# Key-value state and turned query weights through PSUM, large buffers at multiples of 512 bytes, and a new operation list, in a layer of linear attention and gated feed-forward

## The chip, the core and the metric

The kernel runs on one core of a Trainium2 chip. A core has five engines that each work through their own instructions in order: TensorE (PE, matrix products into PSUM, with a second row PEld for its weight loads), VectorE (DVE), ScalarE (ACT), GpSimd (POOL) and SyncE (SP), which here only issues transfers. SBUF is the working memory of 128 partitions; PSUM holds the results of matrix products in eight banks of 128 x 512 float32. The metric is the device time of one execution in microseconds (us); lower is better.

## What is computed

With `xn = layernorm(x)` for 2048 tokens of width 512:

```python
qkv = (xn @ wqkv) -> q, k, v            # 32 heads of 16
phi(t) = [softmax(t @ w_phi), softmax(-t @ w_phi)]        # 32 features per head
kv  = phi(k)^T v                        # per head, 32 x 16
z   = sum over tokens of phi(k)
o   = (phi(q) kv) / (phi(q) z + 1e-6)
s   = o @ wo
g   = silu((relu(xn @ W_gate) * (xn @ W_up)) @ W_down)    # inner width 1376
out = x + s * g
```

## The kernel before

Every matrix product is made in float32 precision from three products of rounded parts: an operand is split into a high part (a rounded copy, made by ScalarE with `activation(..., AF.Copy)`) and a low part (the rest, made by a subtraction on VectorE or GpSimd). The projections and the gate products use block sums in the manner of Strassen (the names P1 to P7 and the six operand blocks A11, S1 and so on).

The work runs in this order. First a front: tokens are loaded, normalised, transposed on TensorE (`pxT`) and split into the large tile XT; the key weights are folded with `w_phi` (`pfold`). Then the keys, values and queries of all tokens, with the sums `pkv` over tokens kept in four PSUM banks. Then the state: the sums are gathered into `kvacc`, turned on TensorE (`pkb`), masked, and split into a high and a low part that lie in XT in the place of block A21 (which the names of the profile therefore call XT). From there TensorE runs the gate products of the first half of the tokens (names ga, gc, gd and the bank `seed`; eleven slices g0 to g10 of the inner width, seven groups of six products each), the down products (`py`) and the query products (`pnum`). In between stand the query steps: fetch and transpose a query tile into a PSUM bank (`pq<-pql`), its bounds (`mx`), shifting (`eq<-pq,mx`), exponentials, sums, normalising, then a turn by VectorE, a split of the turned weights into `pTh` and `pTl`, and two products per query half against the state. After the first half's outputs (`pso`), the second half of the tokens repeats gate, down and query work with code that this change leaves alone (names pa, pb, pc, pd, u, e).

Two things set the order. Up to the end of the first half's gate work it is a list of names, `ORDER` (before line 37 on), which `Plan.run` (line 105) walks through: each name is an operation that issues a few instructions on one engine, and the engines keep this program order. Behind it, the second half is interleaved by a planner's clock (`Clock.pump`). Names in the list that matter here: `Fk0` to `Fk3` fold the key weights, `khN`/`klN` split a fold into its high and low part, `kcN` copies it; `pk1.0` is the first product of key tile 1; `kpN` turns a quarter of the state, `ktN` masks it, `khN_` and `klN_` split it; `qxQ.J` turns half J of query pair Q, `qhQ.J` and `qoQ.J` split it, `qkQ.Ja` multiplies it; `gF.i` is a group of gate products; `put...` stores prepared weights; `xr...` reloads a block of XT for the second half.

Tiles come from rotating sets. PSUM has one bank `seed` and a set of seven (`ps`); a new tile takes a bank over from an older one and its first writer waits until the last reader of the older one is done. SBUF has sets of 2 (`u8`, 8 KB a partition), 24 (`u4`, 4 KB) and 14 (`u2`, 2 KB) buffers. A set is laid out in memory where it is first used. In the kernel before, XT begins at byte 16,896 of a partition and `u2` at 82,432, both multiples of 512; `u8` and `u4` follow some small tiles and begin at 112,832 and 129,216, both 192 bytes past a multiple of 512.

All engine calls go through `InOrder`, so one line (L128 before, L130 after) stands for every instruction in the profile, and they are told apart by the names of their tiles.

Of the kernel before, what the change touches and what calls it, by code (L numbers as in the profile page):

```python
# [38 lines left out]
kc0 ld2 T1 pk0.0 lk3 lv0 lo3 kh2 bn2 kh1 kl1 pk3.0 ld4 kc1 hi1 pw2 kc2 Fk3 lq0 td1 lv1 bi2 pk0.1 ap2 lq1 vh_0
vh_1 vl_0 kl2 sums0 kh3 pk3.1 st4 T2 th1.0 th1.1 lo1 kc3 vh_2 pk0.2 vl_1 pk3.2 pk1.0 kl3 pk0.3 td3 sums1 vl_2  # L40
ep4 hi2 mx0 Fq0 ld5 pk1.1 pw4 Fq1 pk1.2 pk3.3 qh0 tl1.0 ld6 vh_3 sh0 qh1 lo2 pk1.3 pv1.0 ql0 mx3 st5 Fq2 pk2.0
ql1 pv1.1 ex0 ld7 Fq3 qh2 st6 ld9 pk2.1 qh3 mx1 ql2 bi4 ap4 sh1 sm0 lpm pv1.2 ex1 vl_3 pk2.2 sps1 st7 tl1.1 ep5
ql3 pv0.0 sc0 pk2.3 td2 ep7 sps0 ld12 sh3 pv1.3 vh1 pv0.1 pw5 ep6 bi5 td4 ph0 q1.0 th2.0 z0 ex3 pw7 pq1.0 ap5
q2.0 ld10 pv2.0 sm1 sc1 pw6 T5 pv0.2 st9 pq2.0 vl1 ph1 T4 hi5 bi7 sm3 spill0 pv3.0 bi6 ep9 sc3 pv2.1 pv0.3 th2.1
sums2 pl0 ld8 ap6 lo5 pv3.1 ld11 pw9 tl2.0 pv2.2 ap7 hi4 T7 pv3.2 hS2 z1 tl2.1 vh0 th3.0 th3.1 q1.1 mx2 pl1 hi7
st8 lo4 vl0 T6 pq1.1 P1.2 slo2 sh2 sums3 tl3.0 ex2 q2.1 spill1 ep8 cS2 st10 pv2.3 P6.2 pw8 P3.2 hS3 lo7 bankc
sm2 pq2.1 tl3.1 sc2 bankb hi6 slo3 bankd bi9 lo6 sq1.1 ep10 z2 th4.0 banka pw10 pv3.3 ap9 kv0 sq2.0 cU2 vh2 mx4
tl4.0 th4.1 ld13 vl2 bi8 bi10 P7.2 kv1 cW2 P5.2 sh4 ph2 aw2 tl4.1 pl2 vh3 sq2.1 P4.2 z3 vl3 mx5 P2.2 st11 ph3
ap8 ex4 au2 sh5 sm4 P1.3 kv2 q3.0 ap10 cS3 P6.3 ex5 st12 P3.3 sc4 sm5 pq3.0 vh5 sc5 pl3 ep11 T9 pw11 cU3 vl5 hi9
z5 P7.3 T8 mx6 kv3 spill2 cW3 lo9 P4.3 hi8 ph5 spill3 st13 sq1.0 sums4 lo8 hS4 ph4 P5.3 pl5 sh6 ep12 aw3 mx7  # L50
slo4 q3.1 ex6 bi11 pq3.1 ap11 P2.3 pw12 ld15 sh7 P1.4 ex7 sm6 au3 kv5 z4 pl4 cS4 P6.4 vh4 st15 cU4 vl4 sm7 sc6
vh7 sc7 T10 ep15 hi10 ep13 P3.4 P7.4 bi12 z7 vl7 T11 lo10 sums5 pw13 cW4 hi11 kv4 ph7 hS5 P4.4 mx8 lo11 mx9 q4.1
sh9 pq4.1 spS2 pl7 P5.4 aw4 ph6 sh8 bi13 ex9 P1.5 z6 kv7 sm9 P2.4 ld14 cS5 pw15 slo5 au4 P6.5 ex8 ap13 q4.0 P3.5
vh6 sm8 sc8 vh9 st14 cU5 pq4.0 T13 ap12 P7.5 ph8 hi13 sq4.1 sc9 pl6 cW5 spS3 bi15 mx10 T12 vl6 kv6 vl9 hi12 ph9
lo13 sums6 sh10 hS6 lo12 P4.5 z8 ap15 ep14 pl8 z9 mx11 ex10 vh8 q5.1 q5.0 pq5.1 pl9 sm10 slo6 sh11 vl8 pq5.0
sc10 pw14 P5.5 rw0 P1.6 z10 ex11 cS6 aw5 sm11 kv9 P2.5 bi14 fd0 P6.6 rd0 fs0 kv8 ft0 sc11 ap14 T15 au5 ph10 cU6
z11 pl10 T14 hi15 ph11 P7.6 lo15 P3.6 sums7 cW6 mx12 P4.6 vh11 sq3.1 hi14 q6.1 pl11 lo14 mx13 hS7 P1.7 vl11 sh13
pq6.1 kv11 ex13 slo7 cS7 fdl0 sh12 vh10 P5.6 fa0 sm13 P6.7 ex12 P3.7 aw6 rw1 sc13 sm12 P2.6 au6 vl10 kv10 sq5.1
vh13 cU7 ph13 fal0 vl13 fs1 fa1 sq6.1 sc12 fb0 ph12 P7.7 cW7 P5.7 z13 sq3.0 aw7 mx14 vh12 q7.1 fd1 sh14 ft1 P4.7
rd1 mx15 fc0 rw2 pq7.1 P2.7 sq7.1 ex14 q6.0 fbl0 au7 vh14 vl12 fc1 rd2 q8.0 pq6.0 sh15 g0.0 pl13 sm14 sq5.0 fs2  # L60
vh15 sc14 fcl0 ex15 pl12 gt0 sm15 vl15 vl14 kv12 z12 rw3 sq4.0 fs3 g0.1 sq6.0 ph14 sc15 pq8.0 rd3 fb1 q8.1 pq8.1
gm0 g0.2 pl14 kv13 ql0.0 ge0 sq8.0 ql0.1 g0.3 gf0 g0.4 fal1 kv14 g0.5 ph15 fcl1 z15 pl15 g0.6 gp0 fe0 ft2 fbl1
putwa0 gs0 kv15 z14 g1.0 gn0 gg0 fe1 fb2 ka q7.0 qt0.1 g1.1 putwd0 hc0 qm0.1 fel1 kb ft3 kp3 qt0.0 gt1 pq7.0
g1.2 putwa1 fa3 qm0.0 fbl2 ha0 putwb0 fc2 kp1 g1.3 gm1 kt3 ge1 kh3_ fd2 hb0 kp0 qs0.1 fa2 g1.4 kt1 sq7.0 fc3 zp0
fb3 fel0 gf1 qs0.0 sq8.1 kt0 fd3 fe3 fdl1 gp1 qe0.0 g1.5 zc0 fal2 zp1 g1.6 fcl2 ql1.0 kh0_ qt1.0 rw4 gs1 qa0.0
putwb1 kh1_ g2.0 qm1.0 putwc2 g2.1 ha1 of_3 zc1 kl3_ qe0.1 qs1.0 ql1.1 gt2 putfe1 fdl2 gn1 kp2 fel3 putwb2 hd0
g2.2 gg1 fs4 gm2 fdl3 hb1 qt1.1 putwd1 fcl3 putwc1 qe1.0 g2.3 oh_3 hc1 ge2 dn013 kl0_ rd4 kt2 g2.4 fal3 qw0.1
kl1_ fbl3 dn010 kh2_ qm1.1 g2.5 fd4 of_0 qw0.0 hd1 gf2 putwc3 g2.6 fe2 qa0.1 qb0.1 putfe3 putwc0 kl2_ gp2 ow_3
dy010 qs1.1 putwa2 rw5 fa4 gs2 dn012 dy013 g3.0 dn011 os_3 g3.1 qr0 dn000 fal4 dy012 gn2 gt3 g3.2 rd5 qw1.0 fel2
qb0.0 putwa3 dn003 gg2 dy011 fa5 qd0 oh_0 g3.3 dy000 putwa4 ft4 fc4 qa1.0 gm3 ge3 qn0.1 qe1.1 dn002 ow_0 fcl4  # L70
fb4 qx0.1 of_2 gf3 fal5 oh_2 fdl4 qa1.1 g3.4 qn0.0 dn001 qh0.1 g3.5 qx0.0 qh0.0 fbl4 qw1.1 dy003 fs5 putfe0 g3.6
qo0.1 ha2 gp3 gn3 g4.0 rw6 dy001 dy002 putwd3 gt4 qk0.10 qo0.0 ft5 g4.1 qk0.11 fs6 os_0 gg3 qb1.1 gm4 hc3 qc0.10
g4.2 hc2 ge4 fa6 hb2 g4.3 putwd2 qk0.00 qc0.11 g4.4 qb1.0 hd2 hd3 gs3 qr1 rd6 gf4 qk0.01 qd1 g4.5 ow_2 qc0.01
ha3 g4.6 gp4 gn4 dn100 qz0.1 g5.0 rw7 qn1.0 fc5 fd6 fb5 dy100 dn102 fbl5 ql2.0 g5.1 gg4 hb3 qx1.0 gt5 fcl5 fa7
qn1.1 qt2.0 fd5 os_2 dn103 g5.2 of_1 fal7 gm5 dy102 dy103 g5.3 fdl5 putwb4 oh_1 ow_1 ft6 dn101 fs7 fdl6 ge5
qc0.00 putwc5 fc6 rd7 fal6 g5.4 qx1.1 qm2.0 qz0.0 ft7 fb6 dn113 fcl6 dy101 os_1 g5.5 gf5 dn112 qs2.0 putwa5
putwb3 fbl6 dy113 qh1.1 qe2.0 fb7 rw8 putwd4 fd7 fe4 g5.6 qo1.1 gp5 fe5 g6.0 gs5 fel4 qk1.11 g6.1 putwd5 dy112
# [1430 lines left out]
```

## Time and profile before

| | |
|---|---|
| median of 3 runs | 585.66 us (585.11 to 586.7) |
| the profiled execution | 583.23 us |
| its span, first to last instruction | 581.5 us |
| mean granted TensorE clock | 0.991 of full |
| busy PE / PEld / DVE | 561.5 / 462.9 / 427.7 us |
| busy ACT / POOL | 290.0 / 429.6 us |
| moved by transfers | 136.14 MB |

A row of the timeline gives the start (us from the start of the span), the time from the first start to the last end of the merged instructions, engine, line, operation, output<-inputs, shapes, the count, and in brackets how long the engine sat idle before and what ended that. Matrix products are pipelined, so one group's end overlaps the next one's start; their pace is read from start to start. A row of the groups gives busy time and mean ns of one instruction, then the idle time before them. Busy shares of PE are not shares of its peak.

### The profile page before, as it was taken

To read this page: it belongs to the slowest core of one execution; us is meant where nothing else is said; L and a number is where in the kernel's file an instruction comes from. 1 tells how busy PE (TensorE), PEld (TensorE's weight loads), DVE (VectorE), ACT (ScalarE), POOL (GpSimd) and SP (SyncE) were. 2 spreads that over 40 slices of the span, in tenths; PEclk is the share of its full clock that TensorE was granted. 3 is DMA by queue.
4 is the path that set the end of the run, shared out by engine and by line. 5 is a ranking of instruction groups with operands and counts; after the bars stand their busy time and mean duration, and the time that the engine had idled before them with its cause. 6 is when DMAs were issued, how large, how long until landed. Compare 5 with 4: busy or idle time off the path is not lost.

```text
span 581.5 us, 8022 instructions
## 1 busy us (share of the span) xinstructions
PE 561.5 (97%) x2618; PEld 462.9 (80%) x2618; DVE 427.7 (74%) x609; ACT 290.0 (50%) x511; POOL 429.6 (74%) x325
## 2 busy tenths in 40 slices
PE   7899999999999499999979999999999999999997
PEld 6788888888887388888868888878888888888886
DVE  5797898977849998989964543499994969774323
ACT  4899777856547236436353223123564453634510
POOL 1968676879899758879988724362968888888475
PEclk9999999999999789999999999999999999999999
DMA  8654765654786486789899999999666766549883
GB/s 303 233 174 124 185 154 121 143 145 129 215 243 193 161 258 235 227 265 305 305 338 276 346 388 405 399 330 355 176 193 193 235 200 198 169 125 331 223 234 135
DMA packets 81562, 136.14 MB, mean 234 GB/s; under 512 B 7408, under 2 KB 34416, under 8 KB 80624
## 3 DMA queue, kind: packets, MB, share of 16 engines
q1 hardware_dynamic: 77920, 122.97, 63.3%
q0 software_dynamic: 3456, 12.58, 11.4%
q8 instruction: 21, 0.34, 0.2%
q14 instruction: 21, 0.17, 0.1%
q10 hardware_dynamic: 144, 0.07, 0.0%
HBM read 73.47 MB, written 53.74 MB: 219 GB/s over the span
## 4 chain that ended last, share of the span: by engine, by line
PE 89%; issue 3%; DVE 2%; DMA 2%; ACT 2%; POOL 2%; SPq 0%; POOLq 0%; DVEq 0%; ACTq 0%
PE py L128 20%; PE seed L128 9%; PE pa L128 8%; PE pd L128 8%; PE pq L128 8%; PE pso L128 8%; PE pc L128 5%; PE gd L128 5%; PE ga L128 4%; PE gc L128 4%; PE pkv L128 3%; PE pnum L128 3%; PE pv L128 2%; PE pk L128 1%; DMA cb<-cst 1%
## 5 line engine op out<-in xcount | busy, mean ns | idle before, releaser
L128 PE MATMUL py<-fd,hh 128*128 128x512 f32 x528 | 132.8, 395 | 0.0
L128 PEld LDWEIGHTS py<-fd,hh 128*128 128x128 f32 x528 | 100.0, 190 | 22.2
L128 DVE TENSOR_TENSOR y<-py,y 128x512 f32<-128x512 f32 x40 | 26.8, 684 | 24.7 <-PE py L128 24.5
L128 POOL TENSOR_TENSOR phl<-ek,phl 128x1024 fp32r<-128x1024 f32 x16 | 40.5, 2552 | 5.5 <-ACT phl L128 5.5
L128 PE MATMUL pso<-wo,oh 128*128 128x512 f32 (+1 forms) x136 | 39.8, 377 | 0.0
L128 POOL TENSOR_TENSOR ol<-of,oh 128x1024 fp32r<-128x1024 f32 x8 | 19.2, 2400 | 27.6 <-ACT oh L128 17.7
L128 POOL TENSOR_TENSOR ez<-eq,zB 128x1024 f32<-128x1024 f32 x16 | 38.4, 2408 | 0.1
L128 PE MATMUL ga<-XT,wa 128*128 128x512 f32 x132 | 34.4, 396 | 0.0
L128 PE MATMUL pa<-XT,wa 128*128 128x512 f32 x132 | 34.2, 393 | 0.0
L128 PE MATMUL seed<-XT,wb 128*128 128x512 f32 x132 | 34.0, 393 | 0.0
L128 POOL TENSOR_TENSOR y<-y,ys 128x512 f32<-128x512 f32 x24 | 31.1, 1302 | 1.9 <-ACT ys L128 1.9
L128 POOL TENSOR_TENSOR hh<-e,hh 128x512 fp32r<-128x512 f32 x11 | 14.3, 1304 | 24.0 <-ACT hh L128 24.0
L128 DVE TENSOR_TENSOR y<-pso,y 128x512 f32<-128x512 f32 (+1 forms) x15 | 9.8, 656 | 27.6 <-PE pso L128 27.6
L128 PEld LDWEIGHTS pa<-XT,wa 128*128 128x128 f32 x132 | 24.7, 188 | 5.6
L128 PEld LDWEIGHTS ga<-XT,wa 128*128 128x128 f32 x132 | 24.5, 188 | 5.6 <-issue 0.5
L128 PE MATMUL gd<-XT,wc 128*128 128x512 f32 x66 | 18.6, 421 | 10.6 <-DVE eq L128 7.8
L128 PEld LDWEIGHTS seed<-XT,wb 128*128 128x128 f32 x132 | 24.6, 188 | 5.3
L128 PEld LDWEIGHTS pso<-wo,oh 128*128 128x128 f32 x136 | 25.0, 188 | 4.7
L128 ACT ACTIVATE eq<-pnum 128x512 f32<-128x512 f32 x32 | 17.7, 592 | 18.7 <-PE pnum L128 18.7
L128 POOL TENSOR_TENSOR lr<-lr,mhalf 128x1 f32<-128x1 f32 x16 | 9.8, 614 | 22.2 <-DVE lr L128 22.2
L128 ACT ACTIVATE eq<-eq 128x512 f32<-128x512 f32 x32 | 18.4, 623 | 15.2 <-DVE eq L128 15.0
L128 PE MATMUL pso<-wo,ol 128*128 128x512 f32 (+1 forms) x68 | 25.6, 377 | 0.0
(237 smaller groups left out, 1661.5 us busy)
## 6 DMA issues: line engine op xcount, KB each, us to landing
zacc<-ek POOLq DMA_DIRECT2D x16, 512.0 KB, 4.8
XT<-xts SPq DMA_DIRECT2D x7, 1024.0 KB, 17.1
rawg<-wf SPq DMA_DIRECT2D x11, 512.0 KB, 4.9
ws<-wa SPq DMA_DIRECT2D x22, 256.0 KB, 4.6
ws<-wb SPq DMA_DIRECT2D x22, 256.0 KB, 5.7
ws<-wc SPq DMA_DIRECT2D x22, 256.0 KB, 4.8
ws<-fd SPq DMA_DIRECT2D x22, 256.0 KB, 5.6
wa<-ws SPq DMA_DIRECT2D x22, 256.0 KB, 3.1
```

Source lines behind the costliest of these rows:

```text
L128: return self.tc.keep_in_program_order(op(*a, **k))
```

## The change

Four edits.

1. The state. The masked quarter `kvt`, a tile of `u2` in SBUF, goes: the mask is multiplied into the PSUM bank `pkb` in place, and the high copy (ScalarE) and the low subtraction (VectorE) read that bank.
2. The turned query weights of the first half (three query pairs, two halves each). Where VectorE turned 1024 columns from SBUF into a tile `ez` in SBUF, it now turns twice 512 columns into a PSUM bank `pT`; each bank is then split by its own copy on ScalarE and its own subtraction on VectorE.
3. The sets `u8`, `u4` and `u2` are touched right behind XT, before the small tiles, so that they begin at 82,432, 98,816 and 197,120 bytes, multiples of 512.
4. A new `ORDER`, with names for the two parts of each turn.

```diff
+    for buffer in (u8, u4, u2):
+        buffer((P, 512), "first")
...
             def masked():
-                T[t_] = u2((P, 2, P), "kvt")
-                nc.vector.tensor_tensor(T[t_], T[b_], T["pm"][:, 2:4, :], op=ALU.mult)
+                nc.vector.tensor_tensor(T[b_], T[b_], T["pm"][:, 2:4, :], op=ALU.mult)
 
             def high():
-                nc.scalar.activation(kvhl[:, 0, g, :], T[t_], AF.Copy)
-                nc.scalar.activation(quarter(kvhl[:, 1, g, :]), quarter(T[t_]), AF.Copy)
+                nc.scalar.activation(kvhl[:, 0, g, :], T[b_], AF.Copy)
+                nc.scalar.activation(quarter(kvhl[:, 1, g, :]), quarter(T[b_]), AF.Copy)
...
             op(f"kl{i}_", lambda: add(nc.vector, kvhl[:, 1, g, :].rearrange("p q (s c) -> p (q s) c", s=2)[:, 1:3, :],
-                                      quarter(T[t_]), f32(quarter(kvhl[:, 0, g, :])), ALU.subtract), t_)
+                                      quarter(T[b_]), f32(quarter(kvhl[:, 0, g, :])), ALU.subtract), b_)
...
-        def high():
-            T[th] = u4((P, 1024), "pTh", F32R)
-            nc.scalar.activation(T[th], T[ez], AF.Copy)
-
-        def low():
-            T[tl] = u4((P, 1024), "pTl", F32R)
-            add(nc.vector, T[tl], T[ez], f32(T[th]), ALU.subtract)
...
-        op(f"qx{q}.{j}", lambda: nc.vector.transpose(T[ez], flat(T[es])), es, ez)
-        op(f"qh{q}.{j}", high, ez, th)
-        op(f"qo{q}.{j}", low, ez, th, tl)
+
+        def turned(d, p):
+            c = slice(d * 512, (d + 1) * 512)
+
+            def turn():
+                T[p] = ps(name="pT")
+                nc.vector.transpose(T[p], flat(T[es])[:, c])
+
+            def high():
+                if th not in T:
+                    T[th] = u4((P, 1024), "pTh", F32R)
+                nc.scalar.activation(T[th][:, c], T[p], AF.Copy)
+
+            def low():
+                if tl not in T:
+                    T[tl] = u4((P, 1024), "pTl", F32R)
+                add(nc.vector, T[tl][:, c], T[p], f32(T[th][:, c]), ALU.subtract)
+            op(f"qx{q}.{j}{d}", turn, es, p)
+            op(f"qh{q}.{j}{d}", high, p, th)
+            op(f"qo{q}.{j}{d}", low, p, th, tl)
+        for d in range(2):
+            turned(d, f"pT{q}.{j}{d}")
...
 ORDER = """
-ld3 bn3 ld0 pw3 ld1 bn0 bn1 pw0 bi3 ap3 ap0 lk0 lcb T0 pw1 bi1 lk2 Fk0 lk1 T3 Fk2 ap1 hi0 Fk1 lo0 kh0 kl0 hi3
+ld1 ld0 bn1 ld3 bn0 lk0 pw1 bi1 bn3 lcb ap1 lk2 T1 pw0 ap0 pw3 bi3 ap3 T0 Fk0 kh0 sums0 hi1 lk1 lk3 kl0 T3 hi0
```

What the new list moves, at the three places that the prediction speaks of. First VectorE at the state, in the kernel before. `XT<-kvt,XT` is the low subtraction of a state quarter, `kvt<-pkb,pm` the mask, and `eq<-pq,mx` the shifting of a query half, which is the last reader of the bank `pq`.

```order
L128 TENSOR_TENSOR gc<-gc,m 128x512
L128 STREAM_TRANSPOSE pq_2047<-pql 128x512
L128 SCALAR_TENSOR_TENSOR y<-gc,y 128x512
L128 TENSOR_REDUCE qs<-eq 128x64
L128 TENSOR_REDUCE mx<-pq_2047 128x32 x2
L128 TENSOR_TENSOR XT<-kvt,XT 128x128
L128 TENSOR_TENSOR eq<-pq_2047,mx 128x1024
L128 TENSOR_TENSOR m<-gd,m 128x512
```

The same place on VectorE in the changed kernel:

```order
L130 TENSOR_TENSOR gc<-gc,m 128x512
L130 TENSOR_TENSOR XT<-pkb,XT 128x128
L130 SCALAR_TENSOR_TENSOR y<-gc,y 128x512
L130 TENSOR_TENSOR pkb<-pkb,pm 128x256
L130 STREAM_TRANSPOSE pq_2031<-pql 128x512
L130 TENSOR_TENSOR m<-gd,m 128x512
L130 TENSOR_TENSOR pkb<-pkb,pm 128x256
L130 TENSOR_TENSOR XT<-pkb,XT 128x128
L130 SCALAR_TENSOR_TENSOR m<-ga,m 128x512
L130 TENSOR_TENSOR XT<-pkb,XT 128x128
L130 TENSOR_REDUCE mx<-pq_2031 128x32 x2
```

The subtraction of the state reads `pkb` in place of `kvt`, and stands before the transpose that fills the query bank or between it and its bounds, no longer right ahead of the shifting.

Second ScalarE in the front, before. `B21h<-pfold` is the high copy of a key fold (kh2, then kh3), `wkf<-pfold` its full copy (kc), `junk` the statistics of a token tile, `T1h` a split that is needed later.

```order
L128 ACTIVATE wkf<-pfold 128x512
L128 ACTIVATE xt<-xt,lb,lr 128x512
L128 ACTIVATE B12h<-wvr 128x512 x2
L128 ACTIVATE B21h<-pfold 128x512
L128 ACTIVATE junk,lm<-xt 128x512
L128 ACTIVATE junk,lv<-xt,lm 128x512
L128 ACTIVATE T1h<-wkf 128x512 x2
L128 ACTIVATE wkf<-pfold 128x512
```

And in the changed kernel:

```order
L130 ACTIVATE B21h<-pfold 128x512
L130 ACTIVATE wkf<-pfold 128x512
L130 ACTIVATE B21h<-pfold 128x512
L130 ACTIVATE wkf<-pfold 128x512
L130 ACTIVATE B12h<-wvr 128x512
L130 ACTIVATE xt<-xt,lb,lr 128x512
L130 ACTIVATE junk,lm<-xt 128x512
L130 ACTIVATE junk,lv<-xt,lm 128x512
L130 ACTIVATE wkf<-pfold 128x512
```

Both high copies now come ahead of the statistics; in the list the low part kl3 stands before the last full copy kc3, where before it stood behind it.

Third VectorE at the first turned query half, in the changed kernel. `pT<-eq` is a turn of 512 columns into a PSUM bank, `pTl<-pT,pTh` the subtraction that is the bank's last reader.

```order
L130 STREAM_TRANSPOSE pT<-eq 128x512 x2
L130 TENSOR_TENSOR m<-gd,m 128x512
L130 TENSOR_TENSOR pTl<-pT,pTh 128x512
L130 TENSOR_REDUCE qs<-eq 128x64
L130 TENSOR_TENSOR m<-seed,t 128x512
L130 STREAM_TRANSPOSE pT<-eq 128x512
```

And before:

```order
L128 STREAM_TRANSPOSE ez<-eq 128x1024
L128 TENSOR_TENSOR y<-gd,y 128x512
L128 TENSOR_REDUCE qs<-eq 128x64
L128 TENSOR_TENSOR eq<-eq,qr 128x1024
L128 STREAM_TRANSPOSE ez<-eq 128x1024
L128 TENSOR_TENSOR pTl<-ez,pTh 128x1024
```

Where one turn and one subtraction of 1024 columns between SBUF tiles stood, there are now two of each with a PSUM bank between them, and other work of VectorE stands between the turn and the subtraction.

More of the change, by code (lines that the diff above doesn't have):

```diff
@@ L37 @@
 ORDER = """
-ld3 bn3 ld0 pw3 ld1 bn0 bn1 pw0 bi3 ap3 ap0 lk0 lcb T0 pw1 bi1 lk2 Fk0 lk1 T3 Fk2 ap1 hi0 Fk1 lo0 kh0 kl0 hi3
[L39 to L77, printed above, removed]
@@ new lines @@
+ld2 lv0 lo1 Fk2 lo0 Fk1 kc2 kh1 Fk3 hi3 pk1.0 kl1 ld4 pk0.0 kh2 kc0 kh3 bn2 lq0 pk1.1 pw2 kc1 kl2 pk0.1 vh_0 bi2
+pk0.2 kl3 lo3 pk0.3 ap2 st4 mx0 kc3 pk1.2 vh_1 ep4 lq1 sh0 T2 pk3.0 vl_0 td1 hi2 sums1 ex0 lv1 pw4 ld6 pk1.3 Fq0
+lo2 pk3.1 Fq2 qh0 bi4 th1.0 ld5 vh_2 ld7 ql0 qh2 vl_1 pk3.2 Fq1 ql2 pv1.0 pk2.0 tl1.0 ld8 vl_2 Fq3 vh_3 vl_3 sm0
+ap4 pv1.1 pk2.1 st5 qh1 pv1.2 pk3.3 pk2.2 qh3 mx1 sps0 sh1 td3 th1.1 ld9 st6 ld11 ql3 pv1.3 ql1 ex1 T4 ep5 sc0
+ld10 ep6 pk2.3 td2 st7 sm1 pw5 q1.1 bi5 tl1.1 sc1 ld14 z0 pw6 ph0 ep7 mx2 ap5 q2.0 pq1.1 T5 sh2 ld13 pw7 vh1 st8
@@ new lines @@
+hi4 pl0 pq2.0 ph1 bi7 vl1 ex2 td4 sums2 bi6 mx3 hS2 q2.1 ap7 z1 sps1 lo4 pv3.0 q1.0 pq2.1 hi5 sq2.0 sm2 pv3.1
+pv2.0 th2.0 ep8 pv0.0 ap6 pv2.1 slo2 th2.1 pq1.0 pl1 sh3 T6 lo5 pv0.1 ex3 T7 th3.0 pv0.2 sc2 th3.1 sm3 hi6
+spill1 st9 sums3 P1.2 pv0.3 tl2.0 spill0 pv2.2 pv3.2 cS2 hi7 sc3 sq2.1 vh0 st11 spS2 P3.2 bankc lo6 hS3 tl2.1
+bankb tl3.0 lo7 P6.2 banka vl0 cU2 ep9 bankd pw8 pv3.3 tl3.1 kv0 mx4 vh3 th4.0 vl3 th4.1 z3 bi8 ep11 ph3 pv2.3
+slo3 kv1 pw9 sh4 ex4 tl4.0 P7.2 q3.0 cW2 bi9 sm4 tl4.1 vh2 vl2 P4.2 pl3 P5.2 kv3 sq1.0 ap9 sc4 sq1.1 ph2 mx5 ap8
@@ new lines @@
+sq8.1 kp1 fa3 ge1 qm0.1 fe1 putwb1 fcl1 fb2 fdl1 g1.3 kt1 g1.4 fc3 kt0 g1.5 fc2 qs0.1 fel1 z14 ql2.0 kh1_ gf1
+gp1 qe0.0 kp2 rd3 kl1_ fcl2 gs1 fd2 ql1.1 g1.6 kt2 kp3 qt2.0 fbl2 g2.0 ha1 rw4 gn1 kt3 putwa1 putwa0 rd4 fel0
+of_1 kh2_ kh0_ hc0 kl0_ g2.1 gg1 gt2 kl2_ ql1.0 fcl3 fb3 zp1 qm2.0 fdl2 putfe0 g2.2 hb1 putwc0 gm2 zc1 zp0 g2.3
+qa0.0 ge2 putwc3 fal3 rw5 fd4 g2.4 qs2.0 zc0 qt1.0 gf2 qt1.1 g2.5 qm1.0 fbl3 fs4 qs1.0 fe3 qe0.1 putwb3 g2.6 hd0
+gp2 ft4 fa4 gn2 gs2 hc1 oh_1 qw0.1 dn010 g3.0 putwd0 hd1 dy010 kh3_ fd3 putwd1 qb0.1 fdl3 gt3 fs5 putwc1 qm1.1
@@ new lines @@
+putfe7 gt8 dn213 g8.1 fe6 g8.2 putwb8 fs9 putwc8 putfe5 dy213 g8.3 ft9 gm8 qh2.01 qo2.00 gs7 qz1.1 ge8 hd5
+qx2.11 putwd8 qo2.01 dn211 oa0 putwa8 g8.4 qk2.01 fb9 qk2.00 putfe4 fc9 dy211 qc2.01 g8.5 fal9 gf8 dn212 fbl9
+ql3.1 rw10 gp8 fcl9 hd4 qx2.10 qh2.10 qo2.10 dy212 ol1 sg1 sw0 qh2.11 putwd9 fs10 g8.6 qc2.00 qo2.11 g9.0 gt9
+qk2.11 qk2.10 qc2.11 rd10 ft10 sl1 fa10 qc2.10 g9.1 dn210 putwa9 gm9 qz2.0 fc10 fb10 ha7 g9.2 gn8 dn201 qz2.1
+ge9 g9.3 fbl10 hc6 gg8 fcl10 g9.4 g9.5 gs8 sw1 gf9 putwc9 ol2 g9.6 putwb9 gp9 fal10 hb7 dn203 g10.0 hc7 dy201
@@ L92 @@
+fel6 dn310 gs9 dn312 gt10 hc8 wl2 ha8 g10.1 dy210 oa2 hb8 gn9 wl1 fe8 hd6 dn200 hd7 wl0 dy310 fe9 g10.2 gg9 gm10
+xrA11 dn202 ge10 oa1 hc9 g10.3 dy312 xrS2 ha9 dn313 dy203 fe10 dy202 hd8 g10.4 gp10 fel9 fel8 dn303 fd10 g10.5
+dn311 gf10 xrS3 fdl10 gs10 g10.6 dy200 dn300 dy313 xrS1 gn10 xrA22 gg10 ha10 xrS4 dy311 dy300 hd9 xrA12 hb10
+dy303 fel10 hb9 dn302 dn301 wl3 hc10 dy302 putwa10 hd10 dy301 putfe9 putwd10 putwb10 putfe6 putfe8 putfe10
+putwc10
 """
@@ L1067, in kv_part @@
         def kv_part(i):
-            g, b_, t_ = slice(2 * i, 2 * i + 2), f"pkb{i}", f"kvt{i}"
+            g, b_ = slice(2 * i, 2 * i + 2), f"pkb{i}"
             def turn():
```

48 lines of the change are left out of this document (32 added, 16 removed).

## The prediction

> **What bounds the kernel now.** I read the page first, then TensorE's waits, then the timeline at each place where TensorE stops, and last the groups, for the price of each operation that the diff touches. Busy time and the granted clock, from the page:
>
> ```profile
> PE 561.5 (97%) x2618; PEld 462.9 (80%) x2618; DVE 427.7 (74%) x609; ACT 290.0 (50%) x511; POOL 429.6 (74%) x325
> PEclk9999999999999789999999999999999999999999
> ```
>
> TensorE is busy 97% of the span; the span of 581.5 less 561.5 leaves 20.0 us idle in the whole run. No other engine passes 74%. The clock row is low in slices 13 and 14 only, which are 189 to 218 us. Is there anything to gain in the pace itself? The longest stretch of pure products:
>
> ```profile
> 336.31 20.58 PE L128 MATMUL py<-fd,hh 128*128 128x512 f32 x90
> ```
>
> 20.58 / 90 is 229 ns, and a gate group of six takes 1.38 us start to start (below), 230 ns each. So the pace is even, and the change makes no product fewer: a gain must come from idle time. TensorE's waits say where it lies:
>
> ```profile
> PE gd L128 <- DVE eq L128: 7.8, 1, 7.8
> PE gd L128 <- ACT eq L128: 2.8, 1, 2.8
> ...
> PE pnum L128 <- DVE pTl L128: 0.3, 1, 0.3
> ```
>
> One wait of 7.8 us, one of 2.8, and of the turned query weights only 0.3. Here is the first, in TensorE's timeline:
>
> ```profile
> 189.53 1.54 PE L128 MATMUL seed<-XT,wb 128*128 128x512 f32 x6
> 190.91 0.61 PE L128 MATMUL pkb<-pm,kvacc 128*128 128x128 f32 x4
> 191.27 1.64 PE L128 MATMUL gc<-XT,wb 128*128 128x512 f32 x6
> 200.67 2.93 PE L128 MATMUL gd<-XT,wc 128*128 128x512 f32 x6 [7.76 <-DVE eq L128]
> 203.40 2.77 PE L128 MATMUL py<-fd,hh 128*128 128x512 f32 x6
> 205.96 1.80 PE L128 MATMUL gc<-XT,wc 128*128 128x512 f32 x6
> 207.60 0.62 PE L128 MATMUL py<-fd,hh 128*128 128x512 f32 x2
> ```
>
> From seed to the next group it is 190.91 - 189.53 = 1.38, the undisturbed pace. From gc to gd it is 200.67 - 191.27 = 9.40: 8.02 lost. The next three groups take 2.73, 2.56 and 1.64 where 1.38 is due, at the low clock: 1.35 + 1.18 + 0.26 = 2.79 more. The place costs 8.02 + 2.79 = **10.81 us**. What held `eq`, on VectorE:
>
> ```profile
> 188.45 11.03 DVE L128 TENSOR_TENSOR XT<-kvt,XT 128x128 fp32r<-128x128 f32 x1
> 199.41 1.21 DVE L128 TENSOR_TENSOR eq<-pq,mx 128x1024 f32<-128x1024 f32 x1
> ```
>
> `XT<-kvt,XT` is kl2_, one subtraction of 128 columns. It lasts 11.03 us. `eq` queues behind it, is the last reader of a bank of `pq`, and gd needs that bank. And beside it, on GpSimd:
>
> ```profile
> 187.65 1.44 POOL L128 TENSOR_TENSOR tab<-rawg 128x256 f32<-128x256 f32 x2
> ...
> 197.00 2.34 POOL L128 TENSOR_TENSOR ez<-eq,zB 128x1024 f32<-128x1024 f32 x1
> 202.98 1.30 POOL L128 TENSOR_TENSOR hh<-m,hh 128x512 fp32r<-128x512 f32 x1 [3.64 <-ACT hh L128]
> ```
>
> No GpSimd row from 187.65 to 197.00 is marked idle, and the first pause runs from 202.98 - 3.64 = 199.34. The subtraction ends at 188.45 + 11.03 = 199.48. So it stood as long as GpSimd worked without a pause, and ended when the pause came.
>
> **The state, part by part.** The groups price a subtraction with both operands in SBUF, and one with an operand in PSUM:
>
> ```profile
> L128 DVE TENSOR_TENSOR XT<-kvt,XT 128x128 fp32r<-128x128 f32 x4 | 13.1, 3272 | 0.0
> ```
>
> ```profile
> L128 DVE TENSOR_TENSOR y<-py,y 128x512 f32<-128x512 f32 x40 | 26.8, 684 | 24.7 <-PE py L128 24.5
> L128 DVE TENSOR_TENSOR qr<-qr,qd 128x128 f32<-128x128 f32 x8 | 2.4, 299 | 0.3
> ```
>
> `y<-py,y` reads PSUM and SBUF forty times, at all hours of GpSimd, and its mean is a plain 684 ns. `qr`, a bank of PSUM by the code, is the shape at hand: 299 ns for 128 columns. The edit puts `pkb` (PSUM) in the place of `kvt`, so each of the four subtractions should cost 0.3: 13.1 - 4 x 0.3 = 11.9 us off VectorE, of which the 11.03 - 0.3 = 10.7 of kl2_ lay on the path. What is late next? Had kl2_ taken 0.3, `eq` would start at 188.8 and end at 190.0 (1.21 later); gd is due at 191.27 + 1.38 = 192.65. The bank comes 2.7 us ahead, so the stall goes whole, and with it the low clock that followed it: **-10.8**. Bounds: 0 (nothing freed) to -10.81. The mask writes `pkb` in place, and the bank is held until kl, a few more operations; nothing in the trace shows the price, and I put it with the banks below.
>
> The Trainium skill ("SBUF — State Buffer", section "SBUF: two separate sides") says that VectorE with two SBUF inputs and GpSimd exclude each other, the one that starts first holding the ports for one whole instruction. By that, kl2_ could wait for a single GpSimd instruction, 2.34 us at most in these rows; the trace has 11.03, through some nine of them, and the measurement decides. The rule taken at its word is a rival below.
>
> **The front.** TensorE, VectorE and ScalarE at the fold of the keys:
>
> ```profile
> 19.20 0.40 PE L128 MATMUL pk<-B21h,XT 128*128 128x512 f32 x1
> ...
> 21.16 0.50 PE L128 MATMUL pk<-B21l,XT 128*128 128x512 f32 x1 [1.56 <-DVE B21l L128]
> ```
>
> ```profile
> 20.42 0.69 DVE L128 TENSOR_TENSOR B21l<-pfold,B21h 128x512 fp32r<-128x512 f32 x1 [2.08 <-ACT wkf L128]
> ```
>
> ```profile
> 19.81 0.58 ACT L128 ACTIVATE wkf<-pfold 128x512 f32<-128x512 f32 x1
> ```
>
> Start to start 1.96 where 0.23 is due: 1.73 lost to kl3, which on VectorE stands behind kc3's copy on ScalarE, itself behind the statistics and `T1h`. In the new list kl3 stands ahead of kc3, and both high copies ahead of the statistics. I take **-1.7**; bounds 0 (another late operand takes its place) to -1.73.
>
> **The turned query weights.** Price per half, before:
>
> ```profile
> L128 DVE STREAM_TRANSPOSE ez<-eq 128x1024 f32<-128x1024 f32 x16 | 19.8, 1236 | 0.1
> ```
>
> ```profile
> L128 DVE STREAM_TRANSPOSE pq<-pql 128x512 f32<-128x512 f32 x16 | 11.4, 710 | 0.0
> ```
>
> ```profile
> L128 DVE TENSOR_TENSOR pTl<-ez,pTh 128x1024 fp32r<-128x1024 f32 x6 | 9.6, 1601 | 2.4 <-PE pnum L128 1.3 <-ACT pTh L128 0.7 <-PE py L128 0.4
> ```
>
> ```profile
> L128 ACT ACTIVATE pTh<-ez 128x1024 fp32r<-128x1024 f32 x16 | 16.7, 1052 | 1.6 <-POOL wd L128 1.6
> L128 ACT ACTIVATE eq<-pnum 128x512 f32<-128x512 f32 x32 | 17.7, 592 | 18.7 <-PE pnum L128 18.7
> ```
>
> VectorE paid 1236 + 1601 = 2837 ns for each of six halves. Now it pays two turns into PSUM (the `pq` row, 710) and two subtractions from PSUM (the `y` row, 684): 2788. ScalarE paid 1052, and now pays 2 x 592 = 1184 (the `pnum` row reads PSUM). That is 0.3 us less in all on VectorE and 0.8 more on ScalarE, which is busy 50%. TensorE waits 0.3 us in all for `pTl` and never for `pTh`, so I cost this at nothing; the cover is the gate products that stand between. If that cover were gone, a half would gain, not lose: the first bank is turned, copied and subtracted in 710 + 592 + 684 = 1986 ns against 3889 before. Its danger is the bank itself: twelve more tiles go through the set of seven, which is the slower rival.
>
> **Alignment.** No product or wait of before shows its price. The `py` row has both its operands in the buffers that lay 192 past a multiple (`fd` and `hh` are `u4`), while the gate products read XT, which was aligned, and both run at 229 to 230 ns. So I take **0**. One bound is the granted clock: at the low clock six products took 2.56 us, 427 ns each, so full clock could in the end mean half of that, 213. The other bound is no change, as nothing suggests a cost.
>
> **The rest of the new list.** It moves work on every engine. The other large stall, the second of the waits above:
>
> ```profile
> 292.62 1.55 PE L128 MATMUL gc<-XT,wb 128*128 128x512 f32 x6
> 296.95 1.63 PE L128 MATMUL gd<-XT,wc 128*128 128x512 f32 x6 [2.79 <-ACT eq L128]
> ```
>
> 4.33 less 1.38 is 2.95 us, again gd waiting for a query bank. The new list may clear it or have one like it elsewhere, so I take 0, with bounds -3.0 and +3.0.
>
> **The sum**: -10.8 - 1.7 + 0 + 0 + 0 = -12.5. Against the profiled execution's 583.23 that gives 570.7. The median of the runs shown is 585.66, 2.4 above that execution; I take the difference from the median: **573.2 us**.
>
> **Rivals.** (1) *Given back at the reload.* Behind the first half the second half's weights come back through SyncE:
>
> ```profile
> 361.94 1.23 SPq L128 DMA_DIRECT2D wa<-ws  x2
> ```
>
> ```profile
> wa<-ws SPq DMA_DIRECT2D x22, 256.0 KB, 3.1
> ```
>
> ```profile
> 340.00:375.00 35.00, 35.00 (x156) 28.99 (x155) 11.70 (x18) 7.93 (x12) 9.18 (x6) 1.00 1.03 408
> ```
>
> ```profile
> 373.04 1.55 PE L128 MATMUL pa<-XT,wa 128*128 128x512 f32 x6
> ```
>
> They land near 361.94 + 1.23 + 3.1 = 366.3, an estimate; TensorE's window from 340 on is busy for all of its 35.00 us, and `pa<-XT,wa`, the first user, begins at 373.0: the weights are early now. The transfer share there is 1.03, so the transfers may set their own time. If the landing stayed at 366.3 while TensorE came 12.5 early, at 360.5, it would wait 5.8, and the time would be 579.0 (581.8 with 2.8 of low clock as after the first stall). Against it: the chain that leads there starts from TensorE's own last gate groups and moves with them. A new stall of that size made by the list gives the same figure. (2) *Slower: the banks.* A `pT` bank is held from the turn to the second engine's subtraction. Both large waits above are TensorE waiting for a bank to come free, so banks are what is scarce. Twelve tiles at 12.5 / 12 = 1.04 us of wait each eat the gain. If each `pT` subtraction queues behind one `y<-py,y` and one `eq` on VectorE, 0.69 + 1.21 = 1.9 us, and TensorE waits for that bank each time, it is 22.8, so 573.2 + 22.8 = 596.0. Against it: before has many more `pq` and `pnum` banks, and only two of them made TensorE wait over 2.5 us. (3) *The change doesn't do what it says*: the subtraction still reads `kvhl`'s high part from SBUF and writes SBUF, and sticks as before. Then only 1.7 goes: 584.0. By the one-instruction rule read strictly, 2.34 of the 11.03 was the port's and the rest something that stays: 573.2 + 10.8 - 2.3 = 581.7. (4) *Alignment speeds the products*: 229 - 213 = 16 ns on at most 2618 products is 42 us, so about 531. That the aligned XT reads no faster than `py` speaks against it.
>
> By the Trainium skill ("TensorE: Matmul & The Clock Gate", section "Wait — 56ns, not 53.3ns?") such products go back to back at 215.7 ns; at that the saving would be 13 ns each, some 35 us, and no run here shows that pace.
>
> **How the numbers follow.** Forecast 0.66; given back or a new stall of that size 0.15; banks, slower, 0.10; still stuck 0.06; alignment 0.03. The low end is 573.2 less 3.0 (the late stall cleared) less some 2.7 of the smaller idle in the 20.0: 567.5. The high end takes in rival 1 and the strict rule: 582. Outside lie the banks, alignment and part of the stuck case, 0.19 or so. A measurement of this kernel can tell about 0.3% from no change, 1.76 us; faster is thus under 583.9. Forecast, rival 1, alignment and half of rival 3 are faster: 0.87; the other half of rival 3 is the same: 0.03; the banks are slower: 0.10.
>
> **What would show it.** In the changed profile: four `XT<-pkb,XT` near 0.3 us each; gate groups 1.38 apart from 185 to 210; no slice of the clock row under 9; no gap over 1 us in `pk` near 20 us; `pso` running into `pa` without idle time; no wait of TensorE that names `pTl` or `pT` over 1 us; `py` at 229 ns still. The prediction is wrong if an `XT<-pkb,XT` lasts several us, if a bank is waited for at `pT`, if `pa` waits for `wa`, or if the pace of `py` changes.

## The result and the profile after

The changed kernel takes 567.27 us (566.62 to 571.26, four runs) against 586.01 us for the kernel before on the same chip (585.11 to 586.7, four runs): a ratio of 0.9695, 95% interval 0.9655 to 0.9734, 18.7 us faster. The forecast was 573.2, faster by 12.5, in a range from 567.5 to 582.0. The direction holds, and so does the largest term, the state. Taken as it stands, the time lies 0.2 below the range; taken as a ratio of the 585.66 that the forecast started from, it is 567.8 and lies at its low end. Either way some 6 us of gain were not in the forecast, and the experiments look for them.

The profiled execution of the changed kernel took 571.26 us, 12.0 less than the 583.23 of the one before, and is the slowest of its four. Its rows serve for mechanisms; sizes come from the medians. Its page, to set beside the two lines that open the prediction:

```profile
PE 555.1 (97%) x2618; PEld 462.0 (81%) x2618; DVE 414.4 (73%) x621; ACT 289.3 (51%) x517; POOL 423.4 (74%) x325
PEclk9999999999999999998999999999999999999999
```

The two low slices of the clock at 189 to 218 us are gone (one at 256 to 270 is new, behind a wait of `ga` that ends at 261.33), and TensorE's busy time fell by 6.4 us, from 561.5 to 555.1, with the same 2618 products; its idle time fell from 20.0 to 14.4 us. TensorE's waits in the changed kernel:

```profile
PE ga L130 <- POOL wa L130: 2.1, 2, 1.3
PE py L130 <- POOL tab L130: 2.1, 1, 2.1
PE ga L130 <- ACT eq L130: 1.8, 1, 1.8
PE seed L130 <- DVE idle L130: 1.5, 1, 1.5
PE pz L130 <- DMA zacc<-ek: 1.1, 1, 1.1
...
PE pnum L130 <- DVE pTl L130: 0.2, 1, 0.2
```

No 7.8 any more, and `pk` is gone from the list. The 1.5 of `seed` stood there before; the other waits of 1 to 2 us, in the gate part, are new. Those of `ga` and `pz` come with the new list (run 2, which has the same list, shows them too, at 0.9 to 1.7 us in total); the 2.1 of `py` is not in run 2. The subtractions of the state, as the view of the tile `pkb` gives them (minimum, median and maximum in ns), and the third and the fourth of them in VectorE's timeline:

```profile
L130 DVE TENSOR_TENSOR XT<-pkb,XT x4: 279/280/281, 179.3 to 199.5; 128x128 fp32r<-128x128 f32 x4
```

```profile
183.03 0.28 DVE L130 TENSOR_TENSOR XT<-pkb,XT 128x128 fp32r<-128x128 f32 x1
183.23 1.27 DVE L130 TENSOR_REDUCE mx<-pq 128x32 f32<-128x512 f32 x2
...
199.53 0.28 DVE L130 TENSOR_TENSOR XT<-pkb,XT 128x128 fp32r<-128x128 f32 x1
199.72 1.21 DVE L130 TENSOR_TENSOR eq<-pq,mx 128x1024 f32<-128x1024 f32 x1
```

All four take 0.28 us, where one took 11.03. The section on the change says that none of them stands right ahead of the shifting any more; that is not so of the fourth, which does, and takes no longer there. And the pace, in a stretch of the second half's gate products, which the change's code and list leave alone. The columns are the stretch, its length, the busy time and number of instructions of PE, PEld, DVE, ACT and POOL, then clock, transfer share and GB/s. Before:

```profile
400.00:500.00 100.00, 100.00 (x462) 82.78 (x461) 84.31 (x114) 49.84 (x85) 78.07 (x50) 1.00 0.63 196
336.00:356.00 20.00, 20.00 (x90) 16.57 (x89) 9.28 (x14) 5.39 (x7) 4.66 (x3) 1.00 1.02 401
```

And after:

```profile
400.00:500.00 100.00, 100.00 (x469) 83.92 (x468) 81.22 (x108) 50.59 (x86) 82.81 (x54) 1.00 0.63 199
327.00:347.00 20.00, 20.00 (x90) 16.57 (x89) 9.16 (x14) 8.13 (x11) 8.36 (x5) 1.00 1.02 410
```

Neither kernel waits in these 100 us and both run at full clock, yet TensorE gets through 469 products instead of 462: 1.5% faster, where the prediction said that the pace would stay. The second row of each is the `py` stretch on which the prediction rested this. There both kernels count 90 products in 20 us. The two rows of one kernel differ in two things: in what VectorE, ScalarE and GpSimd do (before, they are 84, 50 and 78% busy in the first, 46, 27 and 23% in the second), and in what TensorE does (in the first its groups change every six products or so, the second is one unbroken run of `py`). Which of the two matters is worked out below, under alignment. From the starts of all products of 512 columns, leaving out those with a gap over 260 ns behind them, the mean pace is 230.2 ns before and 227.2 after; on some 2130 of them that is 6.4 us.

### The profile page after: what moved, and what is told of

The parts are those of the page before. It is cut to its first block, busy times and chain, and to the rows that moved or that the text cites. A ratio compares the mean times of both kernels' runs of the same rounds, so it can differ in the third digit from the quotient of the medians.

```text
span 569.5 us, 8025 instructions
## 1 busy us (share of the span) xinstructions
PE 555.1 (97%) x2618; PEld 462.0 (81%) x2618; DVE 414.4 (73%) x621; ACT 289.3 (51%) x517; POOL 423.4 (74%) x325
## 3 DMA queue, kind: packets, MB, share of 16 engines
q0 software_dynamic: 3456, 12.58, 11.1%
## 4 chain that ended last, share of the span: by engine, by line
PE 75%; DMA 10%; POOL 6%; SPq 5%; issue 1%; ACT 1%; DVE 0%; POOLq 0%; ACTq 0%
PE py L130 16%; PE pd L130 8%; PE pa L130 8%; PE seed L130 8%; PE pso L130 8%; PE pq L130 8%; PE pc L130 5%; SPq L130 5%; DMA rawg<-wf 3%; PE pkv L130 2%; DMA ws<-wc 2%; PE pk L130 2%; PE pv L130 2%; PE pnum L130 2%; PE ga L130 1%
## 5 line engine op out<-in xcount | busy, mean ns | idle before, releaser
L130 PE MATMUL py<-fd,hh 128*128 128x512 f32 x528 | 130.4, 390 | 2.7 <-POOL tab L130 2.1
L130 PEld LDWEIGHTS py<-fd,hh 128*128 128x128 f32 x528 | 98.8, 188 | 24.0 <-POOL tab L130 2.5
L130 POOL TENSOR_TENSOR tab<-rawg 128x256 f32<-128x256 f32 x22 | 15.8, 740 | 11.2 <-DMA xts<-sl 8.8
L130 POOL TENSOR_TENSOR pTl<-ez,pTh 128x1024 fp32r<-128x1024 f32 x10 | 24.1, 2408 | 0.0
L130 ACT ACTIVATE hh<-e 128x512 fp32r<-128x512 f32 x11 | 7.0, 633 | 33.6 <-DVE e L130 33.6
```

The lines of the kernel that those rows point to most:

```text
L130: return self.tc.keep_in_program_order(op(*a, **k))
```

## The experiments

Runs 1 to 4, 5 to 8 and 9 to 12 were taken on three chips, each time with the kernel before beside them. Ratios and intervals are against that; where a time of one chip is set against one of another, a microsecond or two means nothing.

**1. The sets alone.** The kernel before, with this and nothing else:

```diff
     pace.shared = XT.name
+    for buffer in (u8, u4, u2):
+        buffer((P, 512), "first")
```

> The kernel before with one edit only, the three sets touched behind XT so that they begin at multiples of 512. Theory A (where the sets begin sets the pace of the products): products of 512 columns go from a mean of 230.2 ns start to start to about 227.2, which is 3.0 ns on some 2130 of them = 6.4 us; about 579.6 us against 586.0, and the state's stall of 8 us before gd is still there. Theory B (the pace comes from the new list or from the turned weights in PSUM): the pace stays at 230 and the time at 586.

Measured: 576.52 us against 585.68, ratio 0.9842 (0.9780 to 0.9903). The pace is 227.2 ns. Its row for the same stretch:

```profile
400.00:500.00 100.00, 100.00 (x469) 83.95 (x468) 85.59 (x114) 51.39 (x87) 80.37 (x52) 1.00 0.61 188
```

The list is the old one, the turns are the old ones, and the 469 products are there: theory A, except that it expected the state's stall to be there still. In the execution profiled here the 11 us subtraction did not occur:

```profile
188.78 0.81 DVE L128 TENSOR_TENSOR XT<-kvt,XT 128x128 fp32r<-128x128 f32 x1
195.55 0.90 DVE L128 TENSOR_TENSOR XT<-kvt,XT 128x128 fp32r<-128x128 f32 x1
196.71 1.05 DVE L128 TENSOR_TENSOR XT<-kvt,XT 128x128 fp32r<-128x128 f32 x1
201.73 0.95 DVE L128 TENSOR_TENSOR XT<-kvt,XT 128x128 fp32r<-128x128 f32 x1
```

The code of the state is that of the kernel before, and all four take three to four times the 0.28 of the PSUM form, but none sticks: each ends 0.15 us after the end of the GpSimd instruction that was running when it began. That is the likely reason why the time fell by 9.2 us and not by 6.4; part of the stall was given back, as `pnum` then waited 3.8 us for ScalarE (`y`).

**2. The change without the sets.** The two added lines taken out of the changed kernel.

> The changed kernel without the touching of the sets, so that u8 and u4 begin 192 bytes past a multiple of 512 again; everything else as changed. Theory A (where the sets begin sets the pace): the pace goes back to about 230 ns, the time to about 567.3 + 6.4 = 573.7. Theory B (list or PSUM turns): the pace stays at 227, the time at 567.

Measured: 573.54 us, ratio 0.9790 (0.9737 to 0.9843), pace 230.2 ns. That is 6.3 above the changed kernel, as expected. So the sets are worth 6.3 us here, all of it in the pace of the products.

**3. The state alone.** The old list can't hold the `pkb` banks for as long as it held `kvt`, so each `kl` stands right behind its `kh`; the code edit is that of the change:

```diff
-                T[t_] = u2((P, 2, P), "kvt")
-                nc.vector.tensor_tensor(T[t_], T[b_], T["pm"][:, 2:4, :], op=ALU.mult)
+                nc.vector.tensor_tensor(T[b_], T[b_], T["pm"][:, 2:4, :], op=ALU.mult)
```

> The kernel before with the state's quarters masked in PSUM and read from there, and with each low subtraction of the state put right behind its high copy in the list (the banks can't be held longer). Theory S (the subtraction with both operands in SBUF is what sticks beside GpSimd): four subtractions near 0.3 us, no wait of gd near 192 us, 586.0 - 10.8 = about 575.2. Rival (still stuck, since the high part and the output lie in SBUF): one subtraction of several us, 583 to 586.

Measured: 573.36 us (573.28 to 574.09), ratio 0.9787 (0.9736 to 0.9837): 12.3 us faster, 10.8 expected, for the edit and the moved subtractions together. All four subtractions take 0.27 to 0.29 us and no wait of 1 us is left at the state.

**4. Its control.** The same moved subtractions, `kvt` in SBUF.

> The control of the run before it: the same moved subtractions, but kvt stays a tile in SBUF. Theory S (two SBUF operands stick as long as GpSimd works without a pause): at least one of the four lasts over 2 us and ends where GpSimd's next pause begins; time between 575 and 592, by where it stands. Rival (it was the place in the list, not the operand): all four near 0.3 us and the same time as with the state in PSUM.

Measured: 578.84 us, ratio 0.9873 (0.9811 to 0.9936); the five runs were 573.58, 577.48, 578.84, 579.21 and 579.46. The profiled execution is the first:

```profile
180.34 0.65 DVE L162 TENSOR_TENSOR XT<-kvt,XT 128x128 fp32r<-128x128 f32 x1
186.85 0.59 DVE L162 TENSOR_TENSOR XT<-kvt,XT 128x128 fp32r<-128x128 f32 x1 [1.73 <-ACT XT L162]
189.70 1.23 DVE L162 TENSOR_TENSOR XT<-kvt,XT 128x128 fp32r<-128x128 f32 x1
197.40 2.05 DVE L162 TENSOR_TENSOR XT<-kvt,XT 128x128 fp32r<-128x128 f32 x1 [0.49 <-ACT XT L162]
```

GpSimd works beside the last of them:

```profile
196.88 2.42 POOL L162 TENSOR_TENSOR ez<-eq,zB 128x1024 f32<-128x1024 f32 x1
199.25 1.36 POOL L162 TENSOR_TENSOR hh<-m,hh 128x512 fp32r<-128x512 f32 x1
```

Same place, same list, one operand in SBUF instead of PSUM: 0.59 to 2.05 us instead of 0.28, 5.5 us in the median, and a spread of 6 us between executions where the PSUM form has 0.8. That GpSimd is the other party is shown inside the kernel before, where one of the four, with both operands in SBUF, falls into a pause of GpSimd (205.56 to 210.37) and is as short as the PSUM form:

```profile
209.69 0.28 DVE L128 TENSOR_TENSOR XT<-kvt,XT 128x128 fp32r<-128x128 f32 x1
```

So the operand makes the subtraction long. The place has a share in the time all the same: this run leaves both operands in SBUF and only moves the subtractions, and it is 6.8 us faster than the kernel before (3.7 to 11.1 by its interval). Of the 12.3 us of run 3, by the medians, 6.8 come with the move and 5.5 with the operand. Where the four slower executions lose their 4 to 6 us isn't shown; the one profiled is the fastest and as quick as the PSUM form, so there the longer subtractions cost nothing.

What theory S had wrong is the length: the last one ends at 199.45, with one GpSimd instruction (ends 199.30), although GpSimd works on; the other three, too, end 0.15 us after the one that was running when they began. The rule that the prediction weighed (the Trainium skill, "SBUF — State Buffer", section "SBUF: two separate sides": the loser waits for one whole instruction) fits this execution; 11.03 through eight instructions, as profiled before, does not fit it. Both occur.

**5. State and sets together, old list, old turns.**

> The kernel before with the state in PSUM (subtractions moved as in the earlier run) and the sets at multiples of 512, but the old list and the old turns. If the two effects add: 573.4 - 6.3 = 567.1 us, the time of the whole change, so that the new list and the turned weights in PSUM would be worth nothing together. Rival (the new list and the turns carry part of the gain): 569 or more.

Measured: 568.88 us against 585.62, ratio 0.9717 (0.9676 to 0.9758). That is 16.7 us of gain without the new list and the PSUM turns. It lies 1.8 us above what adding would give and at the rival's 569, but its interval overlaps that of the changed kernel's 0.9695, so whether list and turns carry the last 2 us is not decided.

**6. The front.** One name moved in the list of run 5, `kl3` ahead of `kc3`.

> The run before it with one name moved in the list: kl3, the low part of the last key fold, ahead of kc3's copy. Theory (the prediction's front term): the wait of pk near 20 us goes, 1.7 us less, 565.4. Rival (something else is late there next): the same time as the run before it.

Measured: 568.12 us, ratio 0.9691 (0.9642 to 0.9739); 0.8 less than run 5, inside the spread of both. The first row of each fence is the first `pk`, the second the first gate product. Run 5:

```profile
11.97 0.48 PE L162 MATMUL pk<-B11h,XT 128*128 128x512 f32 x1
...
153.94 1.52 PE L162 MATMUL ga<-XT,wa 128*128 128x512 f32 x6
```

Run 6:

```profile
14.93 0.48 PE L162 MATMUL pk<-B11h,XT 128*128 128x512 f32 x1
...
154.87 1.52 PE L162 MATMUL ga<-XT,wa 128*128 128x512 f32 x6
```

141.97 us between them against 139.94: 2.0 us less, and the wait of `pk` for `B21l` is gone. The start of the whole moves by more than that from one execution to the next (11.97 and 14.93), which hides it in the time.

**7 and 8. Which set.** As run 5, with `for buffer in (u4,):` or `(u8,):` alone.

> As the run with state and sets, but only u4 (the operands of the products, and what VectorE, ScalarE and GpSimd work on in 1024 columns) is put at a multiple of 512; u8 stays 192 past. If u4 carries it: pace 227.2 ns and 567. If u8 carries it: pace 230 and 573. If each has a share: between.

> The counterpart: only u8 is put at a multiple of 512, u4 stays 192 past. If u4 carries it: pace 230 ns and 573. If u8 carries it: 227 and 567.

Measured: 569.12 us (0.9717, 0.9675 to 0.9760) at 227.2 ns with u4 alone; 576.13 us (0.9831, 0.9789 to 0.9874) at 230.1 ns with u8 alone. The pace goes with u4 alone.

**9 and 10. Which multiple.** As run 5, with some small tiles touched ahead of the sets, so that all three begin 256 or 64 bytes past a multiple of 512:

```diff
+    sb.tile([P, H, 2], F32, tag="mx", bufs=3, name="first")
     for buffer in (u8, u4, u2):
```

```diff
+    small(6, "bs", 2)
     for buffer in (u8, u4, u2):
```

> As the run with state and sets (568.9), with the small tiles mx touched first, so that all three sets begin 256 bytes past a multiple of 512. If the products need whole multiples of 512: pace 230 ns, 575. If a multiple of 256 (or of a smaller power of two) is enough: pace 227.2 and 569.

> The same with the small tiles bs touched first: all three sets begin 64 bytes past a multiple of 512. If 64 is enough: pace 227.2 and 569; then the 192 of the kernel before, three times 64, would have been harmless, which the runs speak against. So I expect 230 ns or more and 575 or more (u2 lies off too now).

Measured: at 256, 571.55 us (0.9756, 0.9718 to 0.9793) and 227.2 ns; at 64, 578.32 us (0.9871, 0.9840 to 0.9901) and 231.0 ns. The same stretch, first for 256, then for 64:

```profile
400.00:500.00 100.00, 100.00 (x469) 83.95 (x468) 80.79 (x107) 50.39 (x86) 82.80 (x54) 1.00 0.62 197
```

```profile
400.00:500.00 100.00, 100.00 (x460) 82.05 (x459) 83.23 (x112) 51.03 (x87) 80.53 (x52) 1.00 0.61 185
```

Whole multiples of 512 aren't needed: 256 does. 64 is at least as bad as 192, though there `u2` lies off as well, which it doesn't in the kernel before. (The 2.7 us that run 9 lies above run 5 are not in the pace, and the intervals of the two ratios overlap; in its profile gd waits 4.0 us near 286 and goes on at the low clock, where run 5 waits 2.9 near 283.) Whether 128 would do wasn't tried.

**11. The turns.** The changed kernel and its list, with `ez`, one copy and one subtraction of 1024 columns per half.

> The changed kernel with the turned query weights back in SBUF: each half turned in one instruction into ez, copied and subtracted in one each, at the later of the two places that the new list has for each. If the turns through PSUM are worth nothing (the prediction): 567 to 568. If they hide a gain (two-operand subtractions of 1.2 to 2.1 us that hold VectorE): 569 to 572. If their banks cost waits: 565.

Measured: 591.12 us, ratio 1.0095 (1.0062 to 1.0128): slower than before by 1%, and some 23 us above the changed kernel. None of the three expectations. TensorE's waits and VectorE's timeline:

```profile
PE pnum L162 <- DVE pTl L162: 12.1, 6, 4.5
```

```profile
298.12 2.27 DVE L162 TENSOR_TENSOR pTl<-ez,pTh 128x1024 fp32r<-128x1024 f32 x1 [7.25 <-POOL wa L162]
```

`pTl` reads only `ez` and `pTh`, so a wait for GpSimd's `wa` is not one for data: it must be for the u4 buffer that `pTl` takes over. Of VectorE's five waits ahead of `pTl`, four (12.7 us) name something that `pTl` doesn't read, one (3.6 us) its input `pTh`. With the turn in SBUF, `ez` holds a buffer of that set until the subtraction is done; through PSUM it is free before the turn. TensorE waits for all six halves; in the profiled executions it idles 26.5 us against 14.4 in the changed kernel, and its busy time is 6.4 us longer, at a mean clock of 0.985 against 0.997. The new list counts on that buffer and on the shorter chain; it was not made for the old turns, and this run does not say what the best list for them would do (run 5 has one at 568.9).

**12. A version that might beat both.** Run 6 with `fe9` behind `qc2.11` in the list.

> State in PSUM, sets at multiples of 512, kl3 ahead of kc3, and in the old list fe9 (a copy on ScalarE that waited for a buffer, with gt8 and the release of a pnum bank queued behind it) put behind qc2.11. If that copy is what holds gd for 3.0 us near 282: 568.1 - 3.0 = about 565, under the changed kernel's 567.3. Rival (the bank is held by something else, or the buffer's wait turns up behind): 568.

Measured: 568.98 us, ratio 0.9711 (0.9684 to 0.9738): no gain over run 6. The wait of gd near 282 is gone, and there is this in its place:

```profile
282.41 0.39 PE L162 MATMUL pnum<-pTl,XT 128*128 128x256 f32 x1 [3.74 <-DVE pTl L162]
```

```profile
280.09 2.27 DVE L162 TENSOR_TENSOR pTl<-ez,pTh 128x1024 fp32r<-128x1024 f32 x1 [3.69 <-POOL tab L162]
```

The copy was only the first in line. The wait for `tab`, a weight preparation on GpSimd that `pTl` does not read, is again one for a buffer: the buffer itself is late, and the next tile that wants one waits just as long. So the changed kernel, at 0.9695, isn't beaten beyond the intervals by any version here.

## Why the prediction was right or wrong

**The state: right.** The forecast took 10.8 us; the edit with its moved subtractions gave 12.3 (interval of its ratio 9.5 to 15.5 us). The place, the queue behind it and the low clock went as forecast, and no new wait of that size came in its place. What the forecast did not see is that the stall hangs on timing too: moving the subtractions alone gave 6.8 of the 12.3 (run 4), and with the sets alone the stall did not occur (run 1). The reading "it stood as long as GpSimd worked without a pause" holds for that one subtraction, not as a rule: in all eight rows of runs 1 and 4, and in two of the other three of the kernel before, the same operands end 0.15 us after the GpSimd instruction that was running when they began. The one of 11.03 ends 0.15 us after the last of eight (the prediction counts some nine). Why it sticks through them and the others do not stays open.

**Alignment: the step that failed.** "The `py` row has both its operands in the buffers that lay 192 past a multiple (`fd` and `hh` are `u4`), while the gate products read XT, which was aligned, and both run at 229 to 230 ns. So I take 0." It is worth 6.3 us. Three things were wrong with the reading. First, the 229 came from 20.58 / 90, which counts the drain of the last product. The next row gives its start:

```profile
356.72 0.39 PE L128 MATMUL pso<-wo,ol 128*128 128x512 f32 x1
```

From start to start it is (356.72 - 336.31) / 90 = 226.8, not the 230 of the gate groups: the two paces were never equal. Second, the gate products were no control. By the code their weights `wa`, `wb` and `wc` lie in `u4`, like `fd` and `hh`; only their other operand, XT, was on the grid. Third, `py` was taken from one unbroken run of 90, and what decides is the place of a product in the sequence. In the kernel before, the groups of six (gate and `py`) have a mean of 230.5 ns from start to start; in the long runs of `py` the first twelve products have 229.4, and from the thirteenth on it is 226.7. In the changed kernel the three figures are 227.2, 226.9 and 226.7. So an average over 90 products hid a cost that falls on the first few, and the prediction's sign, "`py` at 229 ns still", could not show the change.

It looks as if the other engines' work slowed the products, since the long run is also the stretch in which they do least. The same products at the same place in the sequence tell the two apart. Each window here is one group of six `pa<-XT,wa` between two groups of `py`, from its first start to the next group's. Before:

```profile
402.44:403.82 1.38, 1.38 (x7) 1.13 (x6) 1.34 (x3) 1.18 (x2) 0.00 (x0) 1.00 1.08 404
435.77:437.15 1.38, 1.38 (x7) 1.13 (x6) 1.38 (x2) 1.18 (x2) 1.38 (x2) 1.00 0.83 174
```

And after:

```profile
392.50:393.86 1.36, 1.36 (x7) 1.13 (x6) 1.33 (x3) 1.16 (x2) 0.02 (x1) 1.00 0.00 0
425.35:426.71 1.36, 1.36 (x8) 1.13 (x7) 1.36 (x3) 1.17 (x2) 1.36 (x3) 1.00 0.75 179
```

GpSimd rests in the first window of each kernel and works throughout in the second, and the group takes 1.38 us before and 1.36 after either way. Before, the six steps are 233, 236, 229, 231, 227 and 229 ns in the first window and 233, 236, 230, 230, 226 and 230 in the second. The reverse holds too: of the products from the thirteenth of a long run on, the 36 beside which the three engines together do two engines' work or more have 226.6 ns. Over all products whose place (the group ahead, the group and the position in it) occurs four times or more, 1541 of them, a fit with the place held fixed gives each of the three engines 0.1 ns or less. So the sets at 192 bytes past a multiple slow the products that follow a change of group, and the other engines' work shows no effect on it. Why is open; it is not simply the address of a product's own operands, as `pd<-XT,wd`, which has both on multiples of 512, goes at 230.3 before and 226.8 after.

Rival 4, of which this is the small form, was worked out by a full-clock bound of 213 ns and given 0.03; the pace fell to 227, the value of the long runs. The low end of the range was made of the late stall and smaller idle time, not of the pace; that the time came out close to it is luck.

**The front: right in the part, not to be told in the sum.** It took 1.7 us; run 6 has 2.0 between two fixed points, and the changed kernel 139.6 (12.71 to 152.30) against 143.9 before (12.29 to 156.17). Between these points both run 704 products; TensorE idles 1.9 us there before and not at all after, and most of the rest is pace. In the time it can't be told: run 6 lies 0.8 us and the changed kernel 1.6 us below run 5, which has neither front nor list, all within the intervals, and the new list's gate part has waits of its own, those quoted above. "The new list may clear it or have one like it elsewhere" was the right thing to say of the late stall, and should have been said of the front's gain too.

**The turns: the prices right, a use missed.** Costed at nothing, with the prices right (`pT` turns 709 ns, subtractions 680, copies 592, against 710, 684 and 592 in the prediction). What was missed is that they free a u4 buffer, which the new list needs: with the turns back in SBUF it is some 23 us slower (run 11). No run has the PSUM turns in the old list, so what they are worth there isn't shown. The slower rival, that their banks hold TensorE up, did not occur; no wait for `pT` stands among the waits, and `pnum` waits 0.2 us for `pTl`.

**The reload: did not occur.** `pa` follows `pso` in the changed kernel at 363.40, 9.6 earlier than the 373.04 before, without a wait for `wa`.

**The sum.** State 12.3 and sets 6.3 make 18.6, close to the 18.7 of the whole, but they do not add like that: run 5, which has both, gains 16.7. The sets gave 9.2 us on the kernel before, 4.1 on the state alone (by the ratios of runs 3 and 5) and 6.3 in the changed kernel, at some 3 ns of pace each time; the rest is waits that come and go. What list and turns add together, 2.0 us, is inside the intervals. The forecast of 12.5 was 10.8 + 1.7 + 0.

## What to carry to other kernels

A mean over a long run of like products hides a cost that falls on its first few, and a product with one operand in the suspect buffers is no control for one with two. Compare the same product at the same place in the sequence, from start to start, and before blaming the other engines find the same place with and without their work. Here a group of six took 1.38 us with and without GpSimd, and buffers at multiples of 256 bytes made it 1.36, for two lines of code. And a wait for a buffer isn't cured by moving the first operation that meets it: look for who holds the buffer.
